# First keys and queries in half loads, fillers ahead of the first transposes, and the first weight conversions placed later on ScalarE

## The chip, the cores and the metric

The kernel runs on one core of a Trainium2 chip. The metric is the device time of one execution in microseconds. A profile of one more execution shows what each engine did: TensorE (PE, its weight loads apart as PEld), VectorE (DVE), ScalarE (ACT), GpSimd (POOL) and SyncE (SP), whose queue issues nearly all transfers.

## The reference

Three layers follow one another. The first is attention over 2 batches, 8 heads, 768 positions of 64 numbers; each query sees the 4 first keys (sinks) and the 128 keys up to its own. The second is a gated MLP with weights of 64 bits, the third a top-1 expert layer.

```python
scores = scale * np.matmul(q, k.transpose(0, 1, 3, 2))
keep = is_sink | in_window
scores = np.where(keep, scores, -1000000000.0)
a = np.exp(scores - max); a = a / (sum + 1e-09)
x = np.matmul(a, v)                       # -> (1536 tokens, 512)
g = x @ w_gate
y = (g * sigmoid(g) * (x @ w_val)) @ w_out
# then, for tokens with y @ w_skip > 0: one of 8 experts
out = y + gate_w * (np.maximum(y @ w1[e], 0) @ w2[e])
```

## The kernel before

The 1536 tokens are 12 blocks of 128; the 8 heads of a block are 4 pairs. The steps of attention, one call for each pair or block:

- `step_a(j)` turns the keys and queries of one pair (block 0, pair `j` for `j` below 4) with two transposes on TensorE into a PSUM tile `tqk` (two buffers), and ScalarE copies it to `kq`. For a batch's first block GpSimd copies four sink columns.
- `step_b(j)` is the scores: two matmuls into two PSUM tiles `s` (two buffers in all for blocks 0 to 3), on VectorE the mask with a running minimum (L312, shown as CUSTOM_DVE_ANT_0 or ISA), on ScalarE two exponentials (L316).
- `step_d(j)` transposes the probabilities (`tpt`) and ScalarE copies them to `pt`. `step_s` and `step_e` make the block's output and put it, transposed, into `xt` for the MLP.

The MLP begins (L502, tile `gv`) when four blocks are in `xt`; from then on its matmuls and the attention of the later blocks share the engines. Its weights come as 64-bit numbers: `load_w` issues a 512 KB load into one of three staging tiles `st`, and `convert` makes 32-bit weights of it with two activations on ScalarE (L136, L137) and two operations on VectorE (L141, L142). The staging tile is free again after the last of these, and the next load waits for it on SP's queue, with everything issued behind it.

The instructions of an engine run in the order in which a scheduler wrote them when the program was built. It goes by priorities in program order and by costs of its own; `tc.issue_after(x)` asks it to put what follows behind instruction x. Already before the change, the VectorE half of the first four conversions stands behind the first pair's reduction in this way (`begun["DVE"]`).

Fillers are matmuls of 256 columns on the identity matrix whose result nobody reads. `warm(n)` puts n of them in one place; `filler(1)`, at a low priority, is called after each piece of attention up to the first four blocks.

At the start, SP loads the keys of block 0 (256 KB), its queries (256 KB), its values, two weight tiles and so on. GpSimd builds the identity matrix, VectorE the masks.

Of the kernel before, what the change touches and what calls it, by code (L numbers as in the profile page):

```python
# [8 lines left out]
F32 = mybir.dt.float32  # L9
# [3 lines left out]
ACTF = mybir.ActivationFunctionType  # L13
ALU = mybir.AluOpType
PSUM = bass.MemoryType.PSUM
P = 128

@with_exitstack
def build(ctx: ExitStack, tc: tile.TileContext, q, k, v, n_sink, window,
          wg, wv, wo, w_skip, w_gate, w1, w2, out):  # L20
    nc = tc.nc
    B, H, S, D = q.shape
# [19 lines left out]
    KW = W + P  # L42
# [22 lines left out]
    ldp = early.enter_context(tc.tile_pool(name="ldp", bufs=3))  # L65
# [3 lines left out]
    def act_copy(out, in_, scale=1.0):  # L69
        nc.scalar.activation(out=out, in_=in_, func=ACTF.Copy, scale=scale)  # L70

    def lo_of(out, in_, hi, eng=None):
        (eng or nc.vector).tensor_tensor(out=out, in0=in_, in1=hi.bitcast(F32), op=ALU.subtract)  # L73


    qb, kb, vb = {}, {}, {}

    def load_tok(n, src, dst, nm, bufs):
        b, i = divmod(n, NBLK)
        t = ldp.tile([P, H, D], F32, tag=nm, name=nm, bufs=bufs)  # L80
        nc.sync.dma_start(out=t, in_=src[b, :, i * P:(i + 1) * P, :].rearrange("h p d -> p h d"))
        dst[n] = t

    def load_qk(n):
        if n < NB_ALL:
            load_tok(n, k, kb, "qk", 4)
            load_tok(n, q, qb, "qk", 4)

    def load_v(n):
        if n < NB_ALL:  # L90
            load_tok(n, v, vb, "vb", 3)
# [36 lines left out]
    def convert(dst, si):  # L128

        x = (slice(None),) * (len(si.shape) - 1)  # L130
        low, high = si[x + (0,)], si[x + (1,)]
        di = dst.bitcast(I32)


        h16 = si.bitcast(U16)
        nc.scalar.activation(out=low, in_=h16[x + (1,)], func=ACTF.Copy, scale=2.0 ** -13, bias=2.0 ** -14 - 0.5)  # L136
        nc.scalar.activation(out=dst, in_=high.bitcast(F32), func=ACTF.Abs, scale=2.0 ** -112)  # L137
        with ExitStack() as es:
            if "DVE" in begun and converted[0] < 4:
                es.enter_context(tc.issue_after(begun["DVE"]))  # L140
            nc.vector.scalar_tensor_tensor(out=low, in0=high, scalar=-0x80000000, in1=low, op0=ALU.bitwise_and, op1=ALU.bitwise_or)  # L141
        nc.vector.scalar_tensor_tensor(out=di, in0=di, scalar=3, in1=low, op0=ALU.logical_shift_left, op1=ALU.bitwise_or)  # L142

    converted = [0]

    def convert_w():
        if staged:
            convert(*staged.pop(0))
        converted[0] += 1
        load_w()  # L150
# [72 lines left out]
    begun = {}  # L223
    kq = {}

    def new_kq(pr, parts):
        for hl in range(len(parts)):
            kq[hl, pr] = att.tile([P, PW], parts[hl], tag=f"kq{hl}{pr}", name=f"kq{hl}{pr}")
# [4 lines left out]
    def load_sinks(b):  # L233
        st = sm.tile([96, D], F32, tag="vst", name="vst", bufs=1)
        for a in range(3):
            nc.sync.dma_start(out=st[32 * a:32 * a + 32], in_=v[b, :, 0:4, :])
        hi = sm.tile([96, D], F32R, tag="vsh", name="vsh", bufs=1)
        lo = sm.tile([96, D], F32, tag="vsl", name="vsl", bufs=1)
        nc.vector.tensor_copy(hi, st)
        lo_of(lo, st, hi)  # L240
        vs = sm.tile([96, H, D], F32R, tag="vs", name="vs", bufs=1)
        for a in range(3):
            r = slice(32 * a, 32 * a + 32)
            src = lo[r] if a == 1 else hi.bitcast(F32)[r]
            nc.gpsimd.tensor_tensor(out=vs[r], in0=src.unsqueeze(1).to_broadcast([32, H, D]),
                                    in1=bm[r].unsqueeze(2).to_broadcast([32, H, D]), op=ALU.mult)
        vsk[b] = vs

    def two(t, o, step):
        a = t[:, o:o + P]  # L250
        return bass.AP(a.tensor, a.offset, [a.ap[0], [step, 2], [1, P]])

    def whole(n):

        return n < NBLK

    def step_a(j):

        n, pr = divmod(j, NPAIR)
        i = n % NBLK  # L260
        if i == 0 and n <= NBLK:
            new_kq(pr, [F32] if whole(n) else [F32R, F32R])
        t = attp.tile([P, 512], F32, tag="att", name="tqk")
        for a, src in enumerate((kb[n], qb[n])):
            nc.tensor.transpose(out=t[:, a * P:(a + 1) * P], in_=src[:, 2 * pr:2 * pr + 2, :].rearrange("p h d -> p (h d)"), identity=ident)
        o = (i % 2) * W
        src = t[:, 0:2 * P].rearrange("p (a f) -> p a f", a=2)
        if whole(n):
            act_copy(two(kq[0, pr], o, KW - o), src)
        else:  # L270
            hi, lo = (two(kq[hl, pr], o, KW - o) for hl in range(2))
            act_copy(hi, src)
            lo_of(lo, src, hi)
        if i == 0:
            for hl in range(1 if whole(n) else 2):
                c_ = nc.gpsimd.tensor_copy(kq[hl, pr][:, P:W], (kq[hl, pr] if whole(n) else kq[hl, pr].bitcast(F32))[:, 0:4])
                begun.setdefault("POOL", c_.ins)
# [130 lines left out]
    def attention():  # L408

        done = 0  # L410
        step_a(0)
        step_a(1)
        rest = make_masks()
        warm(10)
        step_b(0)
        yield 0
        for j in range(NP_ALL):
            n, pr = divmod(j, NPAIR)
            if pr == 2:
                load_v(n + 1)  # L420
                load_qk(n + 2)
            if j + 2 < NP_ALL:
                step_a(j + 2)
                yield done
            if j == 0:

                with tc.issue_after(begun["DVE"]), tc.issue_after(begun["POOL"]):
                    rest()
            if j == 1:
                load_sinks(0)  # L430
            if j + 1 < NP_ALL:
                step_b(j + 1)
                yield done
            if pr == 0 and n > 0 and n != GS:
                step_e(n - 1)
                done = n
                if n % NBLK == 0:
                    load_sinks(n // NBLK)
                yield done
            step_d(j)  # L440
            yield done
            if pr == NPAIR - 1:
                step_s(n)
                yield done
                if n == GS - 1:
                    step_e(n)
                    done = n + 1
                    yield done
        step_e(NB_ALL - 1)
        yield NB_ALL  # L450

    def warm(n, pool=acqp, tag="acq"):

        if n:
            t = pool.tile([P, 512], F32, tag=tag, name="warm")
            for _ in range(n):
                nc.tensor.matmul(out=t[:, 0:256], lhsT=idle[:, 0:P], rhs=idle[:, 0:256], start=True, stop=True)
# [706 lines left out]
                    put_row(o, x)  # L1164

    load_par()
    load_qk(0)
    load_v(0)
    make_consts()
    load_w()  # L1170
# [82 lines left out]
```

## Time and profile before

| | us |
|---|---|
| median of 3 runs (624.49 to 627.32) | 627.17 |
| the profiled execution | 628.91 |
| its span, first to last instruction | 627.2 |
| TensorE busy | 592.5 (94%) |
| VectorE busy | 443.4 (71%) |
| ScalarE busy | 368.3 (59%) |

In a timeline a row is: start, duration, engine, line, operation, the tiles written and read, their shape, the count, and in brackets how long the engine had been idle and what ended that. Where a row has a count above 1, the duration goes from the first one's start to the last one's end. An engine name with a q (SPq) is the issue of a transfer, not its travel.

[...]

### The profile page before, as it was taken

What the parts mean: (1) busy time and instruction counts of PE and PEld (TensorE: products, weight loads), DVE (VectorE), ACT (ScalarE), POOL (GpSimd) and SP (SyncE); (2) the same over time, 40 slices, a digit from 0 to 9 for tenths busy, and PEclk for the clock granted to TensorE, in tenths of its full rate; (3) what the DMA queues carried; (4) which work ended last, traced back from release to release, by engine and by line L of the source; (5) the groups of instructions that cost most, each with busy time, mean ns of one, the idle gap of its engine ahead of it and who ended that gap; (6) DMA issues with size and microseconds to landing.
All of it is one profiled execution on the core that took longest, in us unless ns stands there. A gap on an engine that the chain in (4) does not pass through costs nothing. (4 is left out here: it accounts for less than half of the span.)

```text
span 627.2 us, 10713 instructions
## 1 busy us (share of the span) xinstructions
PE 592.5 (94%) x3459; PEld 472.1 (75%) x3459; DVE 443.4 (71%) x1092; ACT 368.3 (59%) x863; POOL 192.1 (31%) x275
## 2 busy tenths in 40 slices
PE   5899998989999999999999999999998999999993
PEld 3566766667777878777778999899986777787772
DVE  3778889797546485665654577778748696989961
ACT  4699776876545355545543456657526675866740
POOL 2465352666343041101111030021005343526411
PEclk9999999989999999999999999999997999999998
DMA  8745879554010220100004200023107886968901
GB/s 201 166 142 154 244 243 271 184 169 101 1 34 1 85 52 18 33 15 4 1 1 152 101 30 2 0 67 111 36 35 229 284 262 212 331 210 286 322 9 38
DMA packets 78421, 75.83 MB, mean 121 GB/s; under 512 B 43138, under 2 KB 55426, under 8 KB 78352
## 3 DMA queue, kind: packets, MB, share of 16 engines
q1 hardware_dynamic: 75552, 69.32, 36.9%
q0 software_dynamic: 2512, 5.68, 2.7%
q8 instruction: 32, 0.52, 0.3%
q14 instruction: 37, 0.30, 0.2%
q10 hardware_dynamic: 288, 0.00, 0.0%
HBM read 65.37 MB, written 11.98 MB: 123 GB/s over the span
## 5 line engine op out<-in xcount | busy, mean ns | idle before, releaser
L502 PE MATMUL gv<-xt,ring 128*128 128x512 f32 (+1 forms) x1152 | 226.6, 346 | 0.4 <-DVE th L536 0.4
L502 PEld LDWEIGHTS gv<-xt,ring 128*128 128x128 f32 x1152 | 176.8, 190 | 27.4 <-issue 2.0
L70 ACT ACTIVATE ring<-w 128x512 fp32r<-128x512 f32 x144 | 90.2, 629 | 98.5 <-PE gv L502 72.1
L73 DVE TENSOR_TENSOR ring<-w,ring 128x512 fp32r<-128x512 f32 x108 | 74.6, 692 | 41.6 <-ACT ring L70 41.0
L514 PE MATMUL acc<-ring,hh 128*128 128x512 f32 x288 | 92.8, 402 | 1.0 <-POOL ring L73 0.6
L73 DVE TENSOR_TENSOR w<-stage,w 128x512 fp32r<-128x512 f32 x96 | 88.4, 954 | 6.9 <-ACT w L70 4.6
L70 ACT ACTIVATE w<-stage 128x512 fp32r<-128x512 f32 x128 | 73.0, 626 | 9.5 <-DMA stage<-in_moe_w_dram 5.5
L73 POOL TENSOR_TENSOR ring<-w,ring 128x512 fp32r<-128x512 f32 x36 | 50.0, 1391 | 53.9 <-ACT ring L70 48.5
L514 PEld LDWEIGHTS acc<-ring,hh 128*128 128x128 f32 x288 | 50.8, 188 | 12.8 <-POOL ring L73 1.0
L349 POOL TENSOR_SCALAR_AFFINE_SELECT pt<-pt 128x256 f32<-128x256 f32 x40 | 22.3, 557 | 124.4 <-ACT pt L70 124.4
L73 POOL TENSOR_TENSOR w<-stage,w 128x512 fp32r<-128x512 f32 x32 | 45.2, 1414 | 47.1 <-ACT w L70 25.1
L514 PE MATMUL acc<-ring,hl 128*128 128x512 f32 x144 | 57.3, 399 | 0.0
L316 ACT ACTIVATE p<-p,st 128x132 f32<-128x132 f32 x96 | 38.3, 400 | 29.7 <-DVE st L312 29.4
L924 PE MATMUL yps<-w,hT 128*128 128x512 f32 x192 | 47.1, 399 | 1.0 <-DVE w L73 0.6
L898 PE MATMUL hps<-w,xh 128*128 128x512 f32 x128 | 42.7, 413 | 0.8 <-issue 0.5
L924 PEld LDWEIGHTS yps<-w,hT 128*128 128x128 f32 x192 | 35.3, 188 | 10.4 <-ACTq L972 1.0
L296 PE MATMUL s<-kq 64*128 64x260 f32 (+1 forms) x144 | 38.3, 427 | 3.4 <-DVE st L312 1.6
L537 DVE TENSOR_TENSOR th<-th,gv 128x512 f32<-128x512 f32 (+1 forms) x48 | 26.5, 552 | 19.8 <-PE gv L502 17.6
L685 POOL DMA_INDIRECT xs<-x,pi x12 | 13.2, 1103 | 81.2 <-ACT ring L70 48.6
L70 ACT ACTIVATE hh<-th 128x512 fp32r<-128x512 f32 (+1 forms) x48 | 25.1, 523 | 17.9 <-DVE th L537 17.7
L296 PEld LDWEIGHTS s<-kq 64*128 64x128 f32 x144 | 18.4, 201 | 21.8 <-issue 13.8
L301 DVE COPY_PREDICATED s<-above,s 128x128 f32<-128x128 int32 x80 | 21.6, 290 | 18.5 <-PE s L296 18.2
(180 smaller groups left out, 951.2 us busy)
## 6 DMA issues: line engine op xcount, KB each, us to landing
stage<-in_moe_w_dram SPq DMA_DIRECT2D x128, 256.0 KB
st<-in_moe_w_gate_dram SPq DMA_DIRECT2D x12, 512.0 KB
st<-in_moe_w_val_dram SPq DMA_DIRECT2D x12, 512.0 KB
st<-in_moe_w_out_dram SPq DMA_DIRECT2D x12, 512.0 KB
xs<-trash SPq DMA_DIRECT2D x8, 387.0 KB
qk<-in_k_dram SPq DMA_DIRECT2D x12, 256.0 KB
qk<-in_q_dram SPq DMA_DIRECT2D x12, 256.0 KB
vb<-in_v_dram SPq DMA_DIRECT2D x12, 256.0 KB
```

The source lines that it names most:

```text
L70: nc.scalar.activation(out=out, in_=in_, func=ACTF.Copy, scale=scale)
L73: (eng or nc.vector).tensor_tensor(out=out, in0=in_, in1=hi.bitcast(F32), op=ALU.subtract)
L296: m_ = nc.tensor.matmul(out=ss[h][:, 0:nk], lhsT=x_, rhs=y_, start=m == 0, stop=m == len(terms) - 1)
L301: nc.vector.copy_predicated(ss[h][:, odd * W:odd * W + P], above, ss[h][:, (1 - odd) * W:(1 - odd) * W + P])
L316: nc.scalar.activation(out=p[:, h], in_=p[:, h], func=ACTF.Exp, scale=-1.0, bias=st[:, h:h + 1], accum_out=su[:, h:h + 1])
L349: nc.gpsimd.affine_select(out=d[:, 0], in_=d[:, 1], compare_op=ALU.is_ge, fill=0.0, base=0, pattern=[[0, 2], [1, P]], channel_multiplier=-1)
L502: nc.tensor.matmul(out=ps, lhsT=w_[:, kk * P:(kk + 1) * P], rhs=x_[:, kk, t0 * P:t1 * P], start=kk == 0 and m == 0, stop=kk == KD - 1 and ...
L514: nc.tensor.matmul(out=acc[g, t], lhsT=h_[:, s], rhs=w_, start=c == 0 and m == 0, stop=c == NFC - 1 and m == 2)
L537: nc.vector.tensor_tensor(out=th, in0=th, in1=vp, op=ALU.mult)
L685: d = nc.gpsimd.indirect_dma_start(out=xs[:, :], out_offset=bass.IndirectOffsetOnAxis(ap=pi[:, t], axis=0), in_=x2s[t], in_offset=None, bo ...
L898: nc.tensor.matmul(out=ps[half], lhsT=x_[:, kk, :], rhs=w_[:, kk, :], start=kk == 0 and m == 0, stop=kk == KD - 1 and m == 2)
L924: nc.tensor.matmul(out=y, lhsT=h_[:, c, :], rhs=w_[:, c % 4, :], start=c == 0 and m == 0, stop=c == NF2 - 1 and m == 2)
```

## The change

Four edits, in three places of the text:

- The keys and queries of block 0 are loaded in halves: first heads 0 to 3 of both, then heads 4 to 7 of both. Four transfers of 128 KB take the place of two of 256 KB, in the same tiles.
- Twelve fillers stand ahead of the first transposes, where ten stood between the first transposes and the first scores.
- The ScalarE half of the first four conversions is asked to stand behind the copy of pair 1 (`begun["ACT"]`).

```diff
+    def load_first_qk():
+        for dst in (kb, qb):
+            dst[0] = ldp.tile([P, H, D], F32, tag="qk", name="qk", bufs=4)
+        for h in range(0, H, H // 2):
+            for src, dst in ((k, kb), (q, qb)):
+                nc.sync.dma_start(out=dst[0][:, h:h + H // 2], in_=src[0, h:h + H // 2, 0:P, :].rearrange("h p d -> p h d"))
...
-        nc.scalar.activation(out=low, in_=h16[x + (1,)], func=ACTF.Copy, scale=2.0 ** -13, bias=2.0 ** -14 - 0.5)
-        nc.scalar.activation(out=dst, in_=high.bitcast(F32), func=ACTF.Abs, scale=2.0 ** -112)
+        with ExitStack() as es:
+            if "ACT" in begun and converted[0] < 4:
+                es.enter_context(tc.issue_after(begun["ACT"]))
+            nc.scalar.activation(out=low, in_=h16[x + (1,)], func=ACTF.Copy, scale=2.0 ** -13, bias=2.0 ** -14 - 0.5)
+            nc.scalar.activation(out=dst, in_=high.bitcast(F32), func=ACTF.Abs, scale=2.0 ** -112)
...
-            act_copy(two(kq[0, pr], o, KW - o), src)
+            c_ = nc.scalar.activation(out=two(kq[0, pr], o, KW - o), in_=src, func=ACTF.Copy)
+            if j == 1:
+                begun["ACT"] = c_.ins
...
         done = 0
+        warm(12)
         step_a(0)
         step_a(1)
         rest = make_masks()
-        warm(10)
         step_b(0)
...
     load_par()
-    load_qk(0)
+    load_first_qk()
     load_v(0)
```

The scheduler writes all five engines' orders anew from this. On TensorE, at the start of the program (`tqk` is a pair's keys and queries, `s` its scores, each pair with two), the kernel before has:

```order
L265 MATMUL tqk<-ident,qk 128x128 x4
L457 LDWEIGHTS ident
L457 MATMUL warm<-ident 128x256
...
L296 MATMUL s_198<-kq_158 128x132
L296 MATMUL s_199<-kq_158 128x132
L265 MATMUL tqk<-ident,qk 128x128 x2
L296 MATMUL s_232<-kq_164 128x132
L265 MATMUL tqk<-ident,qk 128x128
```

The changed kernel has at the same place:

```order
L471 LDWEIGHTS ident
L471 MATMUL warm<-ident 128x256
...
L277 MATMUL tqk<-ident,qk 128x128 x5
L310 MATMUL s_202<-kq_173 128x132
L310 MATMUL s_203<-kq_173 128x132
L277 MATMUL tqk<-ident,qk 128x128 x2
L310 MATMUL s_236<-kq_179 128x132
```

The fillers went ahead of the transposes, and a fifth transpose, of pair 2's keys (second half), now stands ahead of pair 0's scores.

On ScalarE, from the copy of pair 0 on (`kq` a copy of keys and queries, `st` and `w` the two activations of a conversion, `p,sums` an exponential, `pt` a copy of transposed probabilities), before:

```order
L70 ACTIVATE kq_158<-tqk 128x2x128
L70 ACTIVATE kq_164<-tqk 128x2x128
L136 ACTIVATE st<-st 128x512
L137 ACTIVATE w_96<-st 128x4x128
L136 ACTIVATE st<-st 128x512
L137 ACTIVATE w_97<-st 128x4x128
L316 ACTIVATE p,sums<-p,st 128x132 x2
L70 ACTIVATE kq_213<-tqk 128x2x128
L316 ACTIVATE p,sums<-p,st 128x132
```

and of the changed kernel:

```order
L281 ACTIVATE kq_173<-tqk 128x2x128
L281 ACTIVATE kq_179<-tqk 128x2x128
L148 ACTIVATE st<-st 128x512
L149 ACTIVATE w_96<-st 128x4x128
L330 ACTIVATE p,sums<-p,st 128x132 x2
L281 ACTIVATE kq_217<-tqk 128x2x128
L330 ACTIVATE p,sums<-p,st 128x132 x2
L70 ACTIVATE pt<-tpt 128x256
L281 ACTIVATE kq_254<-tqk 128x2x128
L70 ACTIVATE pt<-tpt 128x256
L330 ACTIVATE p,sums<-p,st 128x132 x2
```

The conversion of the gate weights (`w_96`) still stands ahead of the first exponentials; that of the val weights (`w_97`) went some twelve instructions back, into block 1.

On VectorE, in block 1, where the val conversion ends (`s_365` and `s_366` are the scores of block 1, pair 1, `s_369` and `s_370` the same two in the changed kernel), before:

```order
L142 SCALAR_TENSOR_TENSOR w_97<-w_97,st 128x4x128
L73 TENSOR_TENSOR ps<-psk,ps 128x32
L301 COPY_PREDICATED s_365<-above,s_365 128x128
L328 COPY psk<-p 128x8
L301 COPY_PREDICATED s_366<-above,s_366 128x128
L312 ISA p,st<-s_365,mask_110 128x132
```

and of the changed kernel:

```order
L315 COPY_PREDICATED s_370<-above,s_370 128x128
L326 ISA p,st<-s_369,mask_110 128x132
L326 ISA st 128x1
L326 ISA p,st<-s_370,mask_110 128x132
L326 ISA st 128x1
L154 SCALAR_TENSOR_TENSOR w_97<-w_97,st 128x4x128
```

The last operation of that conversion moved from ahead of pair 1's reductions to behind them. From about row 390 of TensorE's 2846 on, and likewise on the other engines, the two kernels have the same order again; in the trace of before that place is at 124.8 us.

## Rows read from the trace of the kernel before

**Rows 1.** Table of four stretches of the span, all engines.

```profile
0.00:22.40 22.40, 16.02 (x63) 10.37 (x64) 8.31 (x50) 10.56 (x33) 5.52 (x25) 1.00 0.78 189
22.40:67.60 45.20, 42.53 (x348) 28.26 (x346) 39.75 (x161) 39.32 (x123) 25.75 (x40) 1.00 0.61 160
67.60:145.00 77.40, 70.08 (x359) 51.85 (x359) 66.35 (x146) 57.60 (x136) 37.05 (x45) 0.98 0.73 218
145.00:460.00 315.00, 314.62 (x1929) 263.04 (x1928) 203.74 (x548) 167.41 (x395) 60.37 (x110) 1.00 0.14 40
```

**Rows 2.** Timeline of TensorE at the start, and six fillers later.

```profile
4.85 0.45 PE L265 MATMUL tqk<-ident,qk 128*128 128x128 f32 x1 [4.85 <-DMA qk<-in_k_dram]
6.83 0.90 PE L265 MATMUL tqk<-ident,qk 128*128 128x128 f32 x3 [1.53 <-DMA qk<-in_q_dram]
7.52 2.34 PE L457 MATMUL warm<-ident 128*128 128x256 bf16 x10
9.79 0.81 PE L296 MATMUL s<-kq 64*128 64x132 f32 x4
...
58.06 0.82 PE L468 MATMUL warm<-ident 128*128 128x256 bf16 x6
```

**Rows 3.** Timeline of SP's queue: issues of transfers.

```profile
0.81 0.45 SPq L81 DMA_DIRECT2D qk<-in_k_dram  x1
1.32 0.58 SPq L81 DMA_DIRECT2D qk<-in_q_dram  x1
...
3.81 1.71 SPq L125 DMA_DIRECT2D st<-in_moe_w_gate_dram  x1
...
24.36 0.37 SPq L125 DMA_DIRECT2D st<-in_moe_w_val_dram  x1
```

**Rows 4.** Timeline of ScalarE, 7 to 23 us.

```profile
7.34 0.81 ACT L70 ACTIVATE kq<-tqk 128x256 f32<-128x256 f32 x2 [4.03 <-PE tqk L265]
9.78 0.66 ACT L136 ACTIVATE st<-st 128x512 int32<-128x512 uint16 x1 [1.64 <-DMA st<-in_moe_w_gate_dram]
...
11.34 0.66 ACT L136 ACTIVATE st<-st 128x512 int32<-128x512 uint16 x1 [0.35 <-DMA st<-in_moe_w_val_dram]
...
12.46 0.39 ACT L316 ACTIVATE p<-p,st 128x132 f32<-128x132 f32 x1
...
13.24 0.36 ACT L70 ACTIVATE kq<-tqk 128x256 f32<-128x256 f32 x1
...
14.61 0.38 ACT L70 ACTIVATE pt<-tpt 128x256 f32<-128x256 f32 x1 [0.62 <-PE tpt L342]
...
17.38 0.38 ACT L70 ACTIVATE kq<-tqk 128x256 f32<-128x256 f32 x1 [1.73 <-PE tqk L265]
...
19.01 0.37 ACT L70 ACTIVATE kq<-tqk 128x256 f32<-128x256 f32 x1
```

**Rows 5.** The stretch from the first conversion to 22.39 us, as in rows 1.

```profile
9.78:22.39 12.61, 12.61 (x50) 8.19 (x50) 6.07 (x36) 8.25 (x28) 2.51 (x6) 1.00 0.83 193
```

**Rows 6.** Timelines of VectorE and GpSimd: identity, sink columns, mask, first reduction, conversions.

```profile
1.31 0.28 POOL masks.py:199 TENSOR_SCALAR_AFFINE_SELECT ident<-ident 128x128 f32<-128x128 f32 x1
...
7.78 0.19 POOL L276 COPY kq<-kq 128x4 f32<-128x4 f32 x1 [4.04 <-ACT kq L70]
...
7.91 0.17 DVE L198 TENSOR_SCALAR mask<-small 128x4 f32<-128x4 f32 x1
10.63 0.30 DVE L312 CUSTOM_DVE_ANT_0 p<-s,mask 128x132 f32<-128x132 f32 x1 [2.55 <-PE s L296]
...
23.61 0.68 DVE L142 SCALAR_TENSOR_TENSOR w<-w,st 128x512 int32<-128x512 int32 x1
...
26.06 0.69 DVE L141 SCALAR_TENSOR_TENSOR st<-st 128x512 int32<-128x512 int32 x1
```

**Rows 7.** Two stretches in the MLP's first phase, as in rows 1.

```profile
129.00:132.00 3.00, 0.78 (x4) 0.61 (x4) 3.00 (x7) 1.86 (x5) 0.97 (x1) 0.88 0.72 189
132.00:135.00 3.00, 3.00 (x9) 2.36 (x8) 2.29 (x6) 1.98 (x6) 1.03 (x2) 0.56 0.64 215
```

## The prediction

> **What bounds the kernel now.** I read the table of stretches first [rows 1]. From 145 to 460 us TensorE is busy 314.62 of 315.00 us. Whatever time is won before 145 us reaches the end from there on, and nothing in that stretch is touched. Up to 22.40 us TensorE shows 16.02 us and up to 67.60 us 42.53 of 45.20, but in these two stretches busy is no bound: fillers are counted, and they stand where TensorE would have waited. ScalarE with 39.32 and VectorE with 39.75 of 45.20 us are the full ones between 22.40 and 67.60, where the MLP's first matmul comes. Ahead of 22.40 they had 10.56 and 8.31 us of work. So the first 22 us are a chain with holes, then comes a stretch full on two engines, then (67.60 to 145) a mixed one in which TensorE lacks 7.3 of 77.40 us and the transfers take 0.73 of their engines, then TensorE.
>
> The chain at the start is read from the timelines. The keys land at 4.85, the queries 1.98 us later at 6.83, and the four transposes run at once [rows 2]. The keys of pair 0 are complete at 7.97 (7.78 + 0.19) and the mask at 8.08 [rows 6], but the scores begin only at 9.79, behind the ten fillers [rows 2], and the first reduction at 10.63 [rows 6]. ScalarE meanwhile waited for the gate weights until 9.78, converted them, waited 0.35 us for the val weights, converted those, and came to the first exponential at 12.46 [rows 4]. From 9.78 to 22.39 it is busy 8.25 of 12.61 us [rows 5], so 4.36 us of holes are left in it, the largest 1.73 us ahead of 17.38 [rows 4].
>
> **The change, part by part.**
>
> *The halves.* The queues issue keys and queries 0.51 us apart [rows 3], and they land 1.98 us apart, so the bytes set the pace. Pairs 0 and 1 need the first half of both, 256 KB, as much as the keys alone were: I take 4.85 us for it, 2.0 earlier than 6.83. Bounds: nothing gained, if the second of two small transfers lands as late as the second of two large ones (6.83), and 2.0. SP issues two transfers more, at 0.45 to 0.58 each [rows 3]. The same bytes are ahead of the gate weights as before, so I leave their landing at 9.78; the other bound is 1.0 later, two issues of about 0.5, if SP's queue and not the bytes sets it.
>
> *The fillers.* Ten took 2.34 us, so twelve take 2.8. They need the identity, which is there at 1.59 [rows 6], and end at about 4.4, ahead of the 4.85 at which TensorE could start anyway: the wait for the keys hides them. Without that cover they would cost up to 2.8. Gone from between transposes and scores, they give back 9.79 - 7.97 = 1.8 us [rows 2, 6].
>
> *The fifth transpose* ahead of pair 0's scores needs the second half of the keys. It is the third of four halves, at about 5.9 (half of the 1.98 behind 4.85), when the first copies are still running. Nothing; at most 0.9 if it came as late as 6.83.
>
> *What these two are worth.* Keys of pair 0 complete at 7.97 - 2.0 = 6.0, scores 0.84 us later (9.79 to 10.63), at 6.8; but the mask is there only at 8.08. So the first reduction comes at 8.1 in place of 10.63, and of the 3.8 us won on TensorE 2.5 arrive at VectorE.
>
> *The conversions.* On ScalarE the gate conversion still stands ahead of the first exponentials, and its weights still land at 9.78. A conversion takes 1.12 us to the next instruction (11.34 to 12.46, rows 4). So the first exponential comes at 10.90 in place of 12.46: 1.56 us of the 2.5. This is the step on which I lay most weight: the ScalarE queue and not the keys sets the first exponential. From there I follow the new order with the durations of [rows 4]: two exponentials to 11.68 (12.46 to 13.24 took 0.78), copy of pair 2 to 11.94, two exponentials of pair 1, long reduced, to 12.72, the probabilities of pair 0 and the keys of pair 3 to about 13.4, a hole of 0.6 for the transposes of pair 1, its copy to 14.4, and the exponentials of pair 2 to 15.2. Before, these ended at 19.01. That is 3.8 us earlier with one conversion (1.12) fewer done: 2.7 us net, in which most of the holes are filled. I take 2.3, since block 1's keys and queries arrive when they did and no row shows when that was. Bounds: 0, if the holes only move, and 4.4, if none were left [rows 5].
>
> *The staging tiles.* The val conversion ends on VectorE at 24.29 (23.61 + 0.68), and SP issues the next val load at 24.36 [rows 3, 6]. Now its last operation stands behind the reductions of block 1, pair 1, which ended where the operation at 26.06 began [rows 6]. 26.06 + 0.68 - 2.3 gives 24.4: the tile comes free when it did. Cost nothing while the 2.3 us hold; 2.4 us later for that tile and for what SP issues behind it where they don't. The conversions moved on ScalarE are no work more or less.
>
> *The rest.* From 22.40 to 67.60 both full engines begin 2.3 us earlier on the same work: carried. From 67.60 to 145 the order differs up to 124.8 us, and I find no row from which to price that: I take 0. The nearest row for both bounds is the gap at 129: TensorE busy 0.78 of 3.00 us, then a granted clock of 0.56 of full speed for 3.00 us [rows 7]. [...] Such a gap costs 2.2 + 3.00 x 0.44 = 3.5 us, won if it goes, lost if one more comes.
>
> **The sum.** 628.91 of the profiled execution less 2.3 gives 626.6. That execution stands 1.74 above the median of the runs, 627.17, so against the median: **624.9**. What a measurement of this kernel can tell from no change is about 0.5%, 3.1 us.
>
> **Rivals.**
>
> 1. *The gain stays at ScalarE's wait for the gate weights.* They land 1.0 later, two issues. For it: ScalarE waited 1.64 us for this transfer already [rows 4], and SP's issues had grown to 1.71 us by then [rows 3]. Against it: the bytes are the same. The gain shrinks to 2.3 - 1.0 = 1.3, and with half of the holes moved to some 0.7: 626.5.
>
> [...]
>
> 3. *The gap at 129 us goes.* The new order has the MLP's output matmuls earlier there, and VectorE, busy 3.00 of 3.00 us [rows 7], is what TensorE waits for. 2.3 + 3.5 = 5.8: 621.4. Against it: from 124.8 on the orders are the same.
>
> 4. *Slower: the staging tile comes free later.* If the holes only move (gain 0), VectorE ends the val conversion 2.4 us later, at 26.7, SP's queue stands behind it, each weight load comes later, and in 67.60 to 145, where the transfers are at 0.73 [rows 1], the MLP waits for its weights. It decides if the tile's operation ends after 24.3 and no slack is left up to the first matmul at 67.60. With one more operation of that kind behind (0.68) that is 3.1 to 3.5 us: 630.5. Against it: ScalarE and VectorE, not the transfers (0.61), are full up to 67.60.
>
> **Chances.** The forecast 0.49 (own range 623.3 to 626.5; a quarter of it lies under the bound of 0.5%, at 624.0), rival 1 0.20, rival 2 0.09, rival 3 0.12, rival 4 0.10. Faster by over 0.5%: 0.12 + 0.09 + 0.12 = 0.33. Slower: 0.09, rival 4 with a rest of it within. Same: 0.58. The range leaves out rival 4 and half of rival 3: **620.8 to 628.6**, the upper end the case that the start gives 2.3 and one more gap costs 3.5 (628.4).
>
> **What would show it.** In the changed kernel's timelines: first transposes at about 4.9 us, fillers ended before; first reduction near 8.1, at the mask's end and not at the scores'; first exponential near 10.9 and directly behind a conversion that waited for the gate weights; the exponentials of pair 2 ended near 15.2; the next val load issued near 24.4; the MLP's first matmul near 65.3 in place of 67.6; TensorE full from about 143. Wrong would be: fillers that begin so late that they push the transposes past 5.5; a landing of the gate weights after 10.5; a first MLP matmul at 67 or later in spite of an early start; a second stretch of low clock between 80 and 140 us; or fillers of 110 to 140 ns before 15 us.

## The result, and the profile after

| | before | changed |
|---|---|---|
| median, us | 627.32 (5 runs, 624.49 to 629.25) | 621.40 (5 runs, 619.06 to 623.07) |
| the profiled execution, us | 628.91 | 619.06 |
| its span, us | 627.2 | 617.3 |

The ratio is 0.9887, with a 95% interval of 0.9854 to 0.9921: about 1.1% faster, with 5.9 us between the medians. The two profiled executions differ by 9.85 us, since each lies at an outer end of its runs. Two executions of one kernel differ by several us (the five of before by up to 4.76), so a single profile shows here where time goes, and only the ratios show how much.

The stretches of the changed kernel, to be held against [rows 1]. A row has the stretch, its length, for PE, PEld, DVE, ACT and POOL the busy time with the count of instructions in brackets, then TensorE's granted clock as a share of its full speed, the share of the transfer engines and GB/s:

```profile
0.00:22.40 22.40, 17.71 (x98) 10.72 (x100) 12.56 (x72) 12.33 (x43) 7.85 (x27) 0.85 0.85 201
22.40:67.60 45.20, 43.46 (x338) 28.81 (x335) 39.87 (x151) 40.43 (x121) 22.74 (x39) 1.00 0.71 188
67.60:145.00 77.40, 72.15 (x384) 54.19 (x383) 67.24 (x146) 60.15 (x141) 45.02 (x51) 1.00 0.72 211
145.00:460.00 315.00, 314.57 (x1950) 263.49 (x1949) 200.52 (x553) 163.48 (x384) 52.04 (x102) 1.00 0.13 39
```

Up to 22.40 us TensorE, VectorE and ScalarE got through more instructions (98, 72 and 43 in place of 63, 50 and 33). From 67.60 to 145 TensorE is 2.1 us busier, and the granted clock is 1.00 in place of 0.98. It reads 0.50 from 8.45 to 15.27 us in the changed kernel's profile and from 131.4 to 134.5 in before's; 1.00 and 0.50 are called the higher and the lower level.

The start, in timelines of TensorE, ScalarE and VectorE of the changed kernel, to be held against [rows 2, 4, 6]:

```profile
1.65 2.74 PE L471 MATMUL warm<-ident 128*128 128x256 bf16 x12 [1.65 <-POOL ident masks.py:199]
4.18 0.42 PE L277 MATMUL tqk<-ident,qk 128*128 128x128 f32 x1
5.99 0.55 PE L277 MATMUL tqk<-ident,qk 128*128 128x128 f32 x3 [1.38 <-DMA qk<-in_q_dram]
...
7.12 0.50 PE L310 MATMUL s<-kq 64*128 64x132 f32 x4
...
10.15 0.82 PE L482 MATMUL warm<-ident 128*128 128x256 bf16 x3
...
15.93 0.27 PE L482 MATMUL warm<-ident 128*128 128x256 bf16 x1
...
63.71 0.73 PE L516 MATMUL gv<-xt,ring 128*128 128x512 f32 x2
```

```profile
6.36 0.66 ACT L281 ACTIVATE kq<-tqk 128x256 f32<-128x256 f32 x2 [3.05 <-PE tqk L277]
9.51 0.66 ACT L148 ACTIVATE st<-st 128x512 int32<-128x512 uint16 x1 [2.50 <-DMA st<-in_moe_w_gate_dram]
...
10.63 0.39 ACT L330 ACTIVATE p<-p,st 128x132 f32<-128x132 f32 x1
...
15.23 0.19 ACT L330 ACTIVATION_READ_ACCUMULATOR p<-p,st 128x1 f32 x1
```

```profile
7.60 0.17 DVE L210 TENSOR_SCALAR mask<-small 128x4 f32<-128x4 f32 x1
7.92 0.30 DVE L326 CUSTOM_DVE_ANT_0 p<-s,mask 128x132 f32<-128x132 f32 x1 [0.15 <-PE tqk L277]
...
23.30 0.69 DVE L415 TENSOR_TENSOR rs<-xps,rs 128x512 f32<-128x512 f32 x1 [0.80 <-PE xps L409]
```

The chain is the one that was forecast: reduction at 7.92, 0.15 us behind the mask's end (7.60 + 0.17), ScalarE 2.50 us in wait for the gate weights, exponential at 10.63, those of pair 2 ended by 15.42 (15.23 + 0.19). The first product of block 0 (`rs`) is at 23.30, where before had it at 29.79, and the first MLP matmul at 63.71 in place of 67.64. The two rows of before:

```profile
29.79 0.69 DVE L401 TENSOR_TENSOR rs<-xps,rs 128x512 f32<-128x512 f32 x1
```

```profile
67.64 0.71 PE L502 MATMUL gv<-xt,ring 128*128 128x512 f32 x2
```

Three marks are used from here on: the first exponential, the first MLP matmul (`gv`), and the seventh tanh of the MLP's first phase, at 144.93 us before and at 135.77 in the changed kernel:

```profile
144.93 0.57 ACT L533 ACTIVATE th<-gv 128x512 f32<-128x512 f32 x1
```

```profile
135.77 0.62 ACT L547 ACTIVATE th<-gv 128x512 f32<-128x512 f32 x1
```

From the seventh tanh to the end the profiles of before, of the changed kernel and of e1 to e8 took 481.5 to 484.4 us. So nearly all of the 9.85 us of this pair arises ahead of it: 3.93 up to the first MLP matmul and 5.23 between it and the seventh tanh (77.29 before, 72.06 after); the rest, 0.7, lies behind.

### The profile page after: what moved, and what is told of

Its sections match the earlier page's. It is cut to its first block, busy times and chain, and to the rows that moved or that the text cites. A ratio compares the mean times of both kernels' runs of the same rounds, so it can differ in the third digit from the quotient of the medians.

```text
span 617.3 us, 10711 instructions
## 1 busy us (share of the span) xinstructions
PE 587.1 (95%) x3461; PEld 467.5 (76%) x3461; DVE 439.6 (71%) x1092; ACT 367.8 (60%) x863; POOL 192.2 (31%) x275
## 5 line engine op out<-in xcount | busy, mean ns | idle before, releaser
L73 DVE TENSOR_TENSOR w<-stage,w 128x512 fp32r<-128x512 f32 x96 | 86.5, 933 | 8.1 <-ACT w L70 5.0
L73 POOL TENSOR_TENSOR ring<-w,ring 128x512 fp32r<-128x512 f32 x36 | 48.6, 1352 | 51.4 <-ACT ring L70 47.4
L363 POOL TENSOR_SCALAR_AFFINE_SELECT pt<-pt 128x256 f32<-128x256 f32 x40 | 20.8, 519 | 124.9 <-ACT pt L70 124.9
L310 PE MATMUL s<-kq 64*128 64x260 f32 (+1 forms) x144 | 35.5, 409 | 1.7 <-DVE st L326 0.9
L528 PEld LDWEIGHTS acc<-ring,hl 128*128 128x128 f32 x144 | 27.0, 188 | 6.9 <-DVE hl L555 0.4
L310 PEld LDWEIGHTS s<-kq 64*128 64x128 f32 x144 | 16.9, 190 | 19.2 <-issue 12.2
```

The source lines that it names most:

```text
L310: m_ = nc.tensor.matmul(out=ss[h][:, 0:nk], lhsT=x_, rhs=y_, start=m == 0, stop=m == len(terms) - 1)
L363: nc.gpsimd.affine_select(out=d[:, 0], in_=d[:, 1], compare_op=ALU.is_ge, fill=0.0, base=0, pattern=[[0, 2], [1, P]], channel_multiplier=-1)
L528: nc.tensor.matmul(out=acc[g, t], lhsT=h_[:, s], rhs=w_, start=c == 0 and m == 0, stop=c == NFC - 1 and m == 2)
```

## The experiments

Ratios are to the kernel before, run on the same chip.

**Halves and fillers apart.** e1 is the kernel before with the half loads alone; every engine but SP has the order of before. e2 is the changed kernel with whole loads, in the changed kernel's order.

```diff
# e1, on before            # e2, on changed
-    load_qk(0)            -    load_first_qk()
+    load_first_qk()       +    load_qk(0)
```

e1: 

> Only the half loads are added to the kernel before; the orders on the compute engines are those of before, ten fillers between transposes and scores. Start theory (the earlier start of the chain makes the gain, however it comes about): first transposes 0.8 to 1.0 us earlier, first exponential still near 12.3 behind two conversions, gain at the first MLP matmul under 1 us, time 0 to -1 us. Order theory (the gain in 67 to 145 us is the new order's): the stretch from the first MLP matmul to the seventh tanh stays near 77 us, as in before. Clock theory (fillers ahead of the transposes bring TensorE to the higher level early): fillers at 7 us stay at about 230 ns, the higher level comes near 21 us.

e2: 

> The changed kernel with the keys and queries of block 0 in whole loads; the orders on the compute engines are those of the changed kernel. Start theory: transposes of the queries at about 6.8 in place of 6.0 us, first reduction some 0.5 later, first exponential unchanged near 10.6, since it waits for the gate weights; time 0 to +1 us against the changed kernel, so -5 to -6 against before. Order theory: the stretch from the first MLP matmul to the seventh tanh is 72 us as in the changed kernel. Clock theory: the higher level may come and go elsewhere in the first 16 us, by up to 1.5 us of the first MLP matmul.

e1 measured 1.0004 (0.9974 to 1.0034), e2 0.9901 (0.9872 to 0.9930). The halves do nothing that can be measured in either order. In e1's profile the first exponential comes at 12.13, in e2's at 10.45, without halves no later than the 10.63 with them: ScalarE's wait for the gate weights (to 9.44 and 9.32) covers what the halves win.

**The fillers' size.** e3 is the changed kernel with the first twelve fillers on a 32 by 32 corner of the array; e4 is the changed kernel itself.

```diff
-        warm(12)
+        warm(12, m=32, kk=32)
```

e3: 

> The changed kernel, but its first twelve fillers use 32 rows and 32 columns of the array in place of 128 and 128; their 256 streamed columns, their count and all orders are the same. Clock theory in the form that the amount of the array at work counts: the transposes at 6 us run at the lower level (0.9 us for three), the higher level comes near 20 us, first MLP matmul 1 to 2.5 us later, time +1 to +2.5 us against the changed kernel. Rival (columns streamed are what counts, or the clock is no matter): same as the changed kernel, 0 within 0.7 us.

e4: 

> The changed kernel once more, as reference on this chip. If the profiled pair told the truth, first MLP matmul near 63.7 us and the seventh tanh near 135.7; if it was a lucky one, the gain from 67 to 145 us is nearer 3.5 than 5.1 us. Time -5 to -7 us against before.

0.9917 (0.9882 to 0.9951) and 0.9923 (0.9894 to 0.9953). How much of the array these fillers use makes no difference to the time here.

**Parts of the order.** e5 is the kernel before with `warm(12)` ahead and `warm(10)` gone; e6 the changed kernel without `warm(12)`; e7 the changed kernel with the conversions asked behind pair 0's second exponential; e8 the kernel before with that rule alone.

```diff
# e7 and e8, in step_b
-            nc.scalar.activation(out=p[:, h], ..., func=ACTF.Exp, ...)
+            x_ = nc.scalar.activation(out=p[:, h], ..., func=ACTF.Exp, ...)
+            if j == 0 and h:
+                begun["ACT"] = x_.ins
```

e5: 

> Only the fillers are moved ahead of the first transposes (twelve); whole loads, no rule for the conversions. On ScalarE the order keeps both conversions ahead of the first exponentials. Queue theory (the first exponentials stand behind the conversions on ScalarE, and taking the val conversion out of their way makes the gain at the start): first reduction near 9.0 as without halves, but first exponential still near 12.0 and block 0's output, the first product with the reciprocal sums, only 1 to 2 us earlier than before's 29.8; time -1 to -3 us. Filler theory (the fillers between transposes and scores were the cost): that product near 24.5, time -5 to -6 us.

e6: 

> The changed kernel without the twelve fillers at all; the scheduler writes the orders a little differently. Queue theory: the conversions stand as in the changed kernel, so first exponential near 10.5, first product with the reciprocal sums near 24, first MLP matmul near 64.5, time -5 to -6.5 us. Clock theory: TensorE starts colder, the higher level comes at or after 21 us, first MLP matmul 1.5 us later than in the changed kernel, time -3 to -4.5 us. A difference from both in the stretch from the first MLP matmul to the seventh tanh (72 us in the changed kernel, 77 before) is the order's.

e7: 

> The changed kernel with the first four conversions asked behind pair 0's exponentials in place of behind pair 1's copy; the order puts the gate conversion behind all exponentials of block 0 and the val and out conversions into block 1. Queue theory: first exponential near 8.9, first product with the reciprocal sums 1 to 2 us ahead of the changed kernel's 23.3 to 24.3, first MLP matmul 0.5 to 1.5 us ahead, time -6 to -7.5 us against before. Staging theory (the staging tiles come free later and hold SP's queue): gate tile free near 18 us in place of 15, first MLP matmul no earlier than 64.5, stretch behind it 1 to 3 us longer, time -3 to -5 us.

e8: 

> The kernel before, with whole loads and ten fillers between transposes and scores, but the first four conversions asked behind pair 0's exponentials, where the order has them as in the run before this one. Queue theory: the scores come late as before, at 9.8, first exponential near 11.1 at once behind its reduction, first product with the reciprocal sums near 26.0, 3.5 to 4.5 us earlier than before; time -3 to -5 us. Filler theory: with the fillers in place the gain at the start stays under 1.5 us, time 0 to -1.5 us.

e5: 1.0072 (1.0038 to 1.0106). e6: 1.0005 (0.9974 to 1.0037). e7: 1.0028 (0.9998 to 1.0059). e8: 0.9947 (0.9915 to 0.9979). The change's rule for ScalarE was also built alone, on before: the scheduler writes the program of before with it. So neither edit does alone what both do, and e5, e6 and e7 came out slower than each theory put down for them. With the fillers alone the scheduler puts both conversions ahead of the first copies, as ScalarE's timeline of e5 shows, and the first exponential falls back to 14.79:

```profile
9.73 0.65 ACT L136 ACTIVATE st<-st 128x512 int32<-128x512 uint16 x1 [6.43 <-DMA st<-in_moe_w_gate_dram]
...
11.88 0.64 ACT L137 ACTIVATE w<-st 128x512 f32<-128x512 f32 x1
12.42 0.64 ACT L70 ACTIVATE kq<-tqk 128x256 f32<-128x256 f32 x2
```

**Other numbers of fillers.** e9 and e10 are the kernel before with 6 and 14 fillers in place of 10; e11 the changed kernel with 4 in place of 12; e12 is e8 with 2 in place of 10.

e9: 

> The kernel before with six fillers between the first transposes and the first scores instead of ten; nothing else is edited, no half loads, no rule for ScalarE, no fillers ahead. The scheduler then by itself writes the val conversion behind the first exponentials and into block 1 on ScalarE. Theory A (the place of the val conversion is what counts): first exponential near 10.7 us, first result of block 0 near 24.5, and the time at or below 0.995 of before. Theory B (fillers must stand ahead of the transposes, so that TensorE has its clock and no wait): the gain is at most the four fillers, 0.9 us at the start, ratio 0.998 to 1.000. Theory C (the whole gain is the order that happens to come out for the MLP's first phase): the start is early, but the stretch from the first MLP matmul to the seventh tanh takes anything between 72 and 77 us.

e10: 

> The kernel before with fourteen fillers in place of ten between the first transposes and the first scores. ScalarE begins as before, with both conversions ahead of the first exponentials; the orders of the engines differ later. Theory A: exponentials at 12.5 as before, no gain at the first MLP matmul (67.6 or later by up to 0.9). Theory C: the stretch from there to the seventh tanh falls from 77.3 to about 72 if it depends on the order alone, and the ratio goes to about 0.993; if the stretch depends on how early the attention is, it stays at 77 and the ratio is 1.000 to 1.002.

e11: 

> The changed kernel with four fillers ahead of the first transposes in place of twelve. ScalarE has the gate conversion ahead of the exponentials and the val conversion far behind, as in the changed kernel; the order differs from there on, as one more order of the same start. Theory A: 0.990 to 0.994, as the changed kernel. Theory C: first exponentials at 10.6 as there, and yet a time anywhere from 0.989 to 1.001, set by the first result of block 0 and by the stretch after the first MLP matmul.

e12: 

> The kernel before with two fillers between in place of ten and the ScalarE half of the first four conversions asked to stand behind pair 0's exponentials (the rule that alone gave 0.9947). First exponential near 9 us, first MLP matmul near 61 if the start is what counts, and with a stretch of 72 us to the seventh tanh a time below the changed kernel's, ratio 0.985. Theory C: the first MLP matmul as early as that, and a ratio of 0.99 to 1.00 by the order that comes out.

e9: 0.9960 (0.9933 to 0.9987). e10: 1.0010 (0.9985 to 1.0035). e11: 1.0067 (1.0040 to 1.0094), although its first exponential is at 10.53. e12: 1.0024 (0.9996 to 1.0051). So an early first exponential is not enough, and theory A (the place of the val conversion) falls. The stretch from the first MLP matmul to the seventh tanh takes either 71.7 to 73.3 us or 75.3 and more, and in before and e8, of the longer kind, TensorE waited for VectorE (2.22 us at 129, 2.21 at 122.6), with the lower granted clock behind it (in before 0.56 from 132 to 135 us [rows 7]). This row of before ends the wait:

```profile
131.39 0.69 PE L342 MATMUL tpt<-ident,p 128*128 128x128 f32 x2 [2.22 <-DVE st L312]
```

**The wait at 129 us.** e13 is the kernel before with fourteen fillers directly ahead of the transposes for which TensorE waits there, e14 with one, e15 is e8 with fourteen.

```diff
+        if j == 23:
+            for _ in range(14):
+                nc.tensor.matmul(out=t..., lhsT=idle[:, 0:P], rhs=idle[:, 0:256], start=True, stop=True)
         for h in range(2):
             m_ = nc.tensor.transpose(out=t[:, h], ...)
```

e13: 

> The kernel before with fourteen fillers of 256 columns directly ahead of the two transposes for which TensorE waits 2.22 us at 129 us (pair 23). TensorE's order is otherwise the same; VectorE's and ScalarE's have the same instructions, some twenty of them right behind the gap in another order. Theory C1 (the lower granted clock behind the gap costs by itself): the fillers bridge the wait, the granted clock stays at 1.00 between 129 and 135 us, the nine matmuls behind take 2.33 us in place of 3.67, and the seventh tanh comes 1.3 to 1.5 us earlier after the first MLP matmul (77.3 to about 75.9); ratio 0.998. Theory C2 (the wait on VectorE is all, the clock no matter): no change, 77 us and 1.000. Theory C3 (the 5 us are this one gap and what hangs on it): about 74 us or less, ratio 0.993.

e14: 

> The kernel before with one filler at the same place, which cannot bridge the wait: TensorE's order as before, VectorE's right behind the gap in nearly the same other order as with fourteen. The wait of some 2 us and the lower granted clock behind it remain by every theory; ratio 1.000. If the time falls as with fourteen fillers, the other order behind the gap has done it and not the clock.

e15: 

> The kernel before with the first four conversions on ScalarE behind pair 0's exponentials (alone 0.9947, first MLP matmul at 62.1, 75.3 us from there to the seventh tanh, a wait of 2.21 us at 122.6 with the lower granted clock behind it), and fourteen fillers in that wait. C1: the stretch falls by about 1.5 us to 73.8, ratio 0.992. C2: 0.9947 again. C3: 72 us as in the changed kernel, ratio 0.989 to 0.990, below the changed kernel's 0.991.

e13: 1.0043 (1.0010 to 1.0076). e14: 1.0008 (0.9972 to 1.0043). e15: 0.9988 (0.9958 to 1.0017). The edit missed its aim. TensorE's timeline of e13:

```profile
128.55 0.97 PE L505 MATMUL gv<-xt,ring 128*128 128x512 f32 x3
131.75 2.24 PE L343 MATMUL tpt<-ident 128*128 128x256 bf16 x14 [2.23 <-DVE st L312]
133.78 0.63 PE L345 MATMUL tpt<-ident,p 128*128 128x128 f32 x2
```

The fillers wait as long as the transposes did (2.23 us), though they need no probabilities: what is late is the PSUM buffer of `tpt`, which the reductions of the scores still read. They then add their own 2.24 us. In e15's profile the granted clock stays at 1.00 behind the wait, and the stretch still takes 78.3 us. So neither the lower clock nor this wait alone is the cause.

**The late fillers.** The written orders part the two kinds. Of the 57 fillers of `filler(1)`, the last two stand in before's order behind 120 MLP matmuls, and in the changed kernel's behind two. They write the tile `ft[0]`, which holds one of the two buffers of the pool `acqp`, and the MLP's accumulator of the fourth token tile (`acc`, L514; the tiles from the third on come from this pool too) can't begin until the last filler has been. In before TensorE's output matmuls behind 48 MLP matmuls stand so:

```
L514 MATMUL acc_1095<-ring_107,hh_967 128x512 x2
L514 MATMUL acc_1095<-ring_107,hl_968 128x512
L514 MATMUL acc_1099<-ring_107,hh_967 128x512 x2
L514 MATMUL acc_1099<-ring_107,hl_968 128x512
L514 MATMUL acc_1103<-ring_107,hh_967 128x512 x2
L514 MATMUL acc_1103<-ring_107,hl_968 128x512
```

These are three token tiles with 9 matmuls. The changed kernel has four tiles with 12 there, and 12 behind every further 24 MLP matmuls. Before has 9, 9 and none, then the two fillers and 30 output matmuls in a row, with four transposes of the attention among them:

```profile
115.38 0.39 PE L468 MATMUL warm<-ident 128*128 128x256 bf16 x2
115.83 0.73 PE L514 MATMUL acc<-ring,hh 128*128 128x512 f32 x2
...
124.84 2.95 PE L502 MATMUL gv<-xt,ring 128*128 128x512 f32 x12
```

All kernels of the longer kind so far have this order, e15 too; none of the shorter kind has. At the last of these rows 120 MLP and 48 output matmuls are done, and from there on both kernels have one order. The changed kernel comes to the same place at 117.21:

```profile
117.21 3.04 PE L516 MATMUL gv<-xt,ring 128*128 128x512 f32 x12
```

e16 is the kernel before without the last two fillers; e17 is the changed kernel with four more at the end, of which two fall behind 120 MLP matmuls; e18 is e8 without the last four.

```diff
# e16 on before (e18: 53, on e8)      # e17 on changed
-        filler(1)                    -        filler(1)
+        if pulls <= 55:              +        filler(3 if pulls > 55 else 1)
+            filler(1)
```

e16: 

> The kernel before without the last two of the 57 low-priority fillers; none of the change's edits. The order of all engines is that of before up to the MLP's first phase (TensorE's first 349 matmuls). Then the output matmuls of the fourth token tile stand with those of the other three, twelve behind each 24 MLP matmuls, as in the changed kernel. Theory F (the late fillers hold the fourth accumulator's buffer, and that costs the 5 us): first MLP matmul at 64 to 67.6 as before, seventh tanh some 72 us later in place of 77 to 80, ratio 0.990 to 0.994. Theory S (the start is the gain, the order in the MLP no matter): ratio 1.000, 77 us.

e17: 

> The changed kernel with four low-priority fillers more at the end of the row of them (three in place of one after the last two pieces of attention). The last two then stand behind 120 MLP matmuls, the fourth accumulator begins only there, and 30 output matmuls stand in a row, as in the kernel before; the start is the changed kernel's. Theory F: first MLP matmul at 64 to 65, from there 76 to 78 us to the seventh tanh, ratio 0.998 to 1.001, the gain of the changed kernel all but gone. Theory S: 0.990 to 0.992 as the changed kernel.

e18: 

> The kernel before with the first four conversions on ScalarE behind pair 0's exponentials (0.9947 and 0.9988 with later fillers added), and without the last four of the 57 low-priority fillers, so that none stands behind 120 MLP matmuls. Theory F: first MLP matmul at 62 to 67, seventh tanh 72 us later, ratio 0.985 to 0.992, level with or below the changed kernel. Theory S: 0.995 to 0.999.

e16: 0.9886 (0.9842 to 0.9929), a median of 620.87. e17: 1.0005 (0.9974 to 1.0037). e18: 0.9921 (0.9883 to 0.9958). Theory F held in e16 and e17 and theory S fell: two fillers taken from the kernel before give the whole gain of the change, and two late fillers in the changed kernel take it back. e18 is weaker: its ratio is at the edge of what F gave, its stretch of 75.3 us is not the 72 of F, and its interval overlaps that of e8 (0.9915 to 0.9979).

The view of one line, the low-priority fillers, from 60 to 140 us: count, shortest, median and longest duration in ns, first and last start. In this order: before, changed, e16, e17.

```profile
L468 PE MATMUL warm<-ident x16: 272/273/283, 60.0 to 115.5; 128*128 128x256 bf16 x16
```

```profile
L482 PE MATMUL warm<-ident x9: 272/273/283, 61.5 to 64.4; 128*128 128x256 bf16 x9
```

```profile
L468 PE MATMUL warm<-ident x14: 272/273/283, 60.2 to 67.9; 128*128 128x256 bf16 x14
```

```profile
L482 PE MATMUL warm<-ident x13: 272/273/283, 61.3 to 112.3; 128*128 128x256 bf16 x13
```

The output matmuls alone, in a table of stretches that has only PE and PEld, then the clock and the transfers; first before, then e16:

```profile
90.00:100.00 10.00, 2.34 (x9) 1.62 (x9) 1.00 0.86 241
100.00:110.00 10.00, 0.00 (x0) 0.00 (x0) 1.00 1.02 280
...
115.00:126.00 11.00, 7.77 (x30) 5.41 (x30) 1.00 0.47 156
```

```profile
90.00:100.00 10.00, 3.04 (x12) 2.18 (x12) 1.00 0.87 249
100.00:110.00 10.00, 3.04 (x12) 2.18 (x12) 1.00 0.96 272
...
115.00:126.00 11.00, 3.29 (x12) 2.10 (x12) 1.00 0.65 181
```

The 30 in a row take 7.77 of the 11 us from 115 to 126. In that time the MLP's other matmuls come to 1.16 us, all of them behind 124.8, and the weight loads stop. SP's queue in before, then in e16, the issues into the staging tiles:

```profile
118.09 0.35 SPq L125 DMA_DIRECT2D st<-in_moe_w_out_dram  x1
...
125.72 0.37 SPq L125 DMA_DIRECT2D st<-in_moe_w_gate_dram  x1
```

```profile
119.18 0.35 SPq L125 DMA_DIRECT2D st<-in_moe_w_out_dram  x1
122.72 0.37 SPq L125 DMA_DIRECT2D st<-in_moe_w_gate_dram  x1
```

7.63 us lie between two loads before, 3.54 in e16. VectorE of before then has the conversions in a bunch, ahead of the reductions that TensorE waits for:

```profile
127.06 1.77 DVE L141 SCALAR_TENSOR_TENSOR st<-st 128x512 int32<-128x512 int32 x1
128.94 1.58 DVE L142 SCALAR_TENSOR_TENSOR w<-w,st 128x512 int32<-128x512 int32 x1
130.45 0.68 DVE L536 SCALAR_TENSOR_TENSOR th<-th,gv 128x512 f32<-128x512 f32 x1
131.04 0.28 DVE L312 CUSTOM_DVE_ANT_0 p<-s,mask 128x132 f32<-128x132 f32 x1
```

The first took 1.77 us, while GpSimd was in two subtractions (126.55 to 129.97); the one at 26.06 took 0.69 [rows 6], with GpSimd idle from 25.19 to 26.58. That the subtractions made it longer is the author's reading of these rows and not shown: the one at 80.78 took 0.68, and GpSimd was in a subtraction there too (80.84 to 82.62). That the bunch comes from the pause of the loads is read from the order of these rows; no run changed it alone.

In e16 the wait and the lower clock at 129 us are gone; its stretches, as in rows 1 and 7:

```profile
67.60:145.00 77.40, 72.86 (x380) 54.63 (x379) 68.85 (x153) 61.59 (x144) 42.93 (x49) 1.00 0.79 227
```

```profile
129.00:132.00 3.00, 3.00 (x16) 2.44 (x15) 2.89 (x8) 2.66 (x8) 1.41 (x3) 1.00 0.75 233
132.00:135.00 3.00, 3.00 (x17) 2.14 (x16) 3.00 (x4) 2.45 (x6) 2.16 (x3) 1.00 0.36 110
```

All the kernels side by side. Late is the order with fillers behind 120 MLP matmuls; times are of each one's profile, the stretch is that from the first MLP matmul to the seventh tanh:

| kernel | late | first exponential | first MLP matmul | stretch | ratio |
|---|---|---|---|---|---|
| before | yes | 12.46 | 67.64 | 77.3 | 1 |
| e1 | yes | 12.13 | 67.06 | 77.1 | 1.0004 |
| e17 | yes | 10.47 | 63.39 | 77.6 | 1.0005 |
| e8 | yes | 10.60 | 62.07 | 75.3 | 0.9947 |
| e15 | yes | 10.94 | 66.94 | 78.3 | 0.9988 |
| e14 | yes | 12.14 | 64.03 | 79.8 | 1.0008 |
| e10 | yes | 12.40 | 66.07 | 78.7 | 1.0010 |
| e12 | yes | 9.46 | 71.08 | 76.0 | 1.0024 |
| e13 | yes | 12.43 | 66.60 | 79.4 | 1.0043 |
| e11 | yes | 10.53 | 69.99 | 75.9 | 1.0067 |
| changed | no | 10.63 | 63.71 | 72.1 | 0.9887 |
| e2 | no | 10.45 | 64.52 | 72.7 | 0.9901 |
| e3 | no | 10.53 | 64.44 | 71.8 | 0.9917 |
| e4 (changed) | no | 10.58 | 64.83 | 72.1 | 0.9923 |
| e16 | no | 12.47 | 67.91 | 72.1 | 0.9886 |
| e18 | no | 10.96 | 62.47 | 75.3 | 0.9921 |
| e9 | no | 11.59 | 69.97 | 71.7 | 0.9960 |
| e6 | no | 10.54 | 68.30 | 72.6 | 1.0005 |
| e7 | no | 8.79 | 73.14 | 73.3 | 1.0028 |
| e5 | no | 14.79 | 75.64 | 71.8 | 1.0072 |

None of the kernels with the late order comes below 0.994; those without it that reach the MLP by 68 us all lie at 0.989 to 0.992. The 68 us were chosen with the table in view, and e6, at 68.30, has 1.0005. On the whole a later first MLP matmul goes with a longer time in each of the two groups. A straight line fitted to the table's 20 rows, an estimate, puts the late order at 0.7% (4.5 us) and each us of a later first MLP matmul at 0.11% (0.7 us); single kernels lie some 0.3% off it, e16 0.7% below.

## Why the prediction was right and wrong

- **The direction and the range** held: 621.4 lies in 620.8 to 628.6. The forecast, 624.9 by a gain of 2.3 us, was the wrong case: its own range ends at 623.3, and it gave 0.58 to a change too small to tell, while the interval ends at 0.9921. The gain is 5.9 us between the medians and has another cause.
- **The start** went as described, row by row: reduction 7.92 (forecast 8.1), exponential 10.63 (10.90), pair 2's exponentials ended at 15.42 (15.2). The step "the ScalarE queue and not the keys sets the first exponential" is shown by e1 and e2. The size of one term was off: the halves bring the queries' transposes to 5.99 and not to 4.85, 0.84 us of the 2.0; it cost nothing, since the first exponential waits for the gate weights anyway. The MLP's first matmul came at 63.71 and not at 65.3.
- **The staging tile**: the next val load was issued at 22.17 (forecast 24.4), so rival 4's delay did not arise, nor rival 1's: the gate weights landed at 9.51.
- **The first failed step** is "From 22.40 to 67.60 both full engines begin 2.3 us earlier on the same work: carried", with the opening sentence that whatever is won before 145 us reaches the end. In the runs that cross start and order it can't be seen: e17 has the changed kernel's start, first MLP matmul at 63.39, and ends at 1.0005; e16 has the start of before and ends at 0.9886, as the changed kernel. That does not make an early start worthless. e8, with the late order and its first MLP matmul at 62.07, has an interval wholly below 1 (0.9947), and by the line through the table the 3.93 us of this start would be worth some 2.8. How much of it reaches the end is open; the gain of this change comes without it. Where e17 gives its gain back is seen in the profile only in part: the stretch is as long as before's (77.6), yet its profiled execution, the fastest of its twelve at 625.71, still has the seventh tanh 3.9 us earlier (141.01).
- **The second failed step** is "From 67.60 to 145 the order differs up to 124.8 us, and I find no row from which to price that: I take 0." The place of the last two fillers in that stretch, taken alone, is worth the whole gain (e16, 0.9886). The trace of before had such a row: two low-priority fillers at 115.4 and 115.5 us, where all the others had ended by 68, and output matmuls in nines and then thirty in a row. The order of both kernels showed the accumulator's place as well.
- **Rival 3** (the gap at 129 us goes, 621.4) came to the measured time, with a chance of 0.12. Its mechanism was one link of the chain. What spoke against it, that "from 124.8 on the orders are the same", was true and beside the point: the cause stands at 115.5. It was also over-sized. From the place where the orders meet (124.84 before, 117.21 after) to the seventh tanh the two profiles take 20.09 and 18.56 us, so the part in which the wait and the lower clock lie, priced at 3.5, gives 1.5 of the 5.23 us of this pair; 3.7 arise ahead of that place (57.20 against 53.50 from the first MLP matmul). In e16 it is 2.6 and 2.6. So that the measured time is the one of this rival is luck in part.
- **Rival 2** (0.09) stands for TensorE at its full clock early, as the clock theory of the experiments does. It came about in part, and nothing shows for it. In the changed kernel's profile the granted clock rose to the higher level at 5.03 us, behind the twelve fillers and one transpose, in the wait for the queries, and stood there up to 8.45: the four score matmuls at 7.12 took 0.50 us, where before's took 0.81. Then it was 0.50 up to 15.27 (256 columns took 421 ns one by one), though TensorE was busy 6.63 of those 6.82 us, and 1.00 from there on (272 ns). e4, the same kernel, had the lower level until 19.66 us (a single filler at 16.39 took 420 ns), though TensorE was busy without a gap from 8 us on, and gained as much (0.9923). What moves the level is not shown, and no ratio shows a price for either.

Open: e6, without late fillers and with a first MLP matmul at 68.30, measured 1.0005, where e16 at 67.91 measured 0.9886. Their profiles read alike (spans 622.4 and 621.8), but e6's profiled execution is the fastest of its twelve and e16's the slowest of its six; what the usual execution of e6 does was not seen. Nor is it settled why e18, with the earliest first MLP matmul of the kernels without the late order, takes 75.3 us for the stretch; ScalarE waits 5.6 us for gate weights there between 64 and 140 us, and 3.7 in the changed kernel.

## What to carry to other kernels

A filler that filled a hole here also held its PSUM buffer until its last use (the fourth tile's accumulator began at 115.83 us, behind the fillers of 115.38), so drop the last of them: two of 57 cost 1.1%. A buffer of their own, for which nobody waits, should do the same; no run tried it. Where a scheduler writes the order, an edit at the start is also an edit of everything behind it; compare the written orders of the busiest engine through to the place where they agree again, and look for tiles whose first use has moved, before a stretch is called carried. And cross the parts (new start with old order, old start with new order), since the profile's differences at the start looked like the cause here, and two fillers alone made the same gain without them.

## What the runs showed of the hardware that was not expected

- The order alone moved the time by 1.9%, from 0.9886 (e16) to 1.0072 (e5), with the same work to within a few fillers.
- In two profiles the granted clock reads 1.00 ahead of the first change. In the changed kernel's that change is at 5.03 us, and the row says 1.00 from the start, while the twelve fillers of 256 columns up to 4.39 us take 228 ns each (2.74 us), the lower level. In the profile of e4, the same kernel, it reads 1.00 until 19.66 us, with single fillers at 420 ns until past 16 us. Durations tell the level there, the row does not.
- Two executions of one program had TensorE's level change at different times: 5.03, 8.45 and 15.27 us in the changed kernel's profile, 19.66 alone in e4's, up to 22 us.
- A 128x512 operation on VectorE took 1.77 us beside GpSimd's subtractions (126.55 to 129.97 us, before), another beside one 0.68 (at 80.78), and one with GpSimd all but idle 0.69 (at 26.06).
